# Gated loads and merged attention events in a decay-attention and softplus-FFN kernel

## The chip, the cores and the metric

The kernel runs on 1 core of a Trainium2 chip. The metric is the device time of one execution in microseconds, the median of several runs. Before the change it is 607.69 us (three runs, 607.14 to 608.19).

## The reference

An attention with exponential decay, without softmax, computed in blocks of 64 positions with a carried state, feeds a two-layer network with a softplus between the layers. All is float32: q, k and v are 4 x 8 x 768 x 64 (batch, heads, positions, size of a head), the network maps 512 to 2048 to 512 for 3072 tokens.

```python
for b in range(nb):
    qb, kb, vb = q[:, :, sl], k[:, :, sl], v[:, :, sl]
    intra = np.einsum('bhic,bhjc->bhij', qb, kb) * Dmask[None]
    intra = np.einsum('bhij,bhjd->bhid', intra, vb)
    inter = np.einsum('bhid,bhde->bhie', qb * lam_pow[None], kv_state)
    out[:, :, sl] = intra + inter
    kb_dec = kb * rev_pow[None]
    kv_state = lam_block[None, :, None, None] * kv_state + np.einsum('bhsd,bhse->bhde', kb_dec, vb)
...
h = x @ w_in
g = np.maximum(h, 0.0) + np.log1p(np.exp(-np.abs(h)))
return (g @ w_out).astype(np.float32)
```

## The kernel before

**Units and chunks.** Positions go in 6 chunks of 128, heads in 4 pairs; a chunk and a pair make one of 24 attention *units* (`NG`), unit g being pair g % 4 of chunk g // 4. Each has its q, k, transposed k and v in one tile of 1 MB, loaded by two transfers of 512 KB (L84, `load_upto`). For a unit, `k_decay` (ACT) and `q_decay` (DVE) scale the inputs; `mm_scores` on PE makes the scores x and the state increments y in 64x64 matmuls (L307, L309); `mask_scores` on DVE (L334) multiplies by the decay mask; `update_states` on DVE (L339) carries the states. `mm_out` (L322, L326) then makes the output in `z`, which `x_high` (ACT, L371) and `x_low` (DVE, L378) split into a high and a low part.

**The network.** It goes in 96 steps, one for each of 16 slices of the 2048 hidden features in each of 6 chunks. `mlp1(s)` (L406) makes h for step s by twelve 128x512 matmuls (4 pairs, three products of high and low parts); `chain_act`, `chain_hi` (ACT, L387, L391) and `chain_lo` (DVE, L395) take the softplus and split it; `mlp2` (L423) of the same step, twelve matmuls more, comes four steps later (`LAG`) and adds into four output banks of its chunk. At a chunk's end the banks are copied out (L429) and stored (L431).

**Weights.** There are 32 raw weight blocks of 512 KB (L126, `w_load`), in the order of `w_order`: first the inner weights of steps 0 to 3, then outer and inner ones in turn. Each is rounded and split on the chip, two at a time in the loop: `w_scale`, `w_round` (ACT, L213, L217), `w_shift`, `w_sign`, `w_add` (DVE, L221, L225, L231), then, one step later, `w_hi` (ACT, L234) and `w_lo` (DVE, L238). Blocks 2s and 2s + 1 begin at step s; the last pair begins at step 15. `w_lo` at step s finishes the outer weight that `mlp2` of step s - 3 needs.

**Order.** The order of the instructions on each engine is that of the program; waits between engines are put in where tiles are shared. Up to step 3 of the loop the order is a list written out by hand (L461 to L473): `xy p` is `mm_scores` of unit p, `a` the mask, `st` the copy of its states, `dg` and `sl` carry them, `z` is `mm_out`, `warm n` is n idle matmuls, `load n` and `unit n` call `w_load(n)` and `load_upto(n)`. All loads are issued by SP in the order of the program; an issue waits there until its tile is free.

**The loop** (L485 on) runs over s from 4. In each step, in the order of the program: the decays of a unit whose event is at s + 1; softplus and split of step s - 1; `w_hi` of the old pair of weights, `w_scale` and `w_round` of the new one, `w_lo` of the old, `w_shift`, `w_sign`, `w_add` of the new; `mlp2` of step s - 4; the attention events; `mlp1(s)`; the loads. Events are of three kinds:

- separate scores (`scores_at`, steps 6, 9, 12 and 17 for units 5 to 8): scores and masks lie in the two banks of `work`;
- separate outputs (`outs_at`, steps 5, 8, 11 and 14 for units 4 to 7);
- both at once (`both_at`, from step 19 every four steps, for the scores of units 9 to 23 and the outputs of the unit before): `mm_out(g - 1)` goes into `work`, and x and y take the two banks of pool `h`, which `mlp1` uses too; a second `mlp2` of the next slice follows, and the next step has none.

The accumulators take all eight PSUM banks: four of `o`, two of `work`, two of `h`.

```python
def work(name):
    return ps.tile([128, 2, 512], F32, tag="t", bufs=1, name=name)
def bank(name):
    return ps.tile([128, 512], F32, tag="h", bufs=2, name=name)
```

Of the kernel before, what the change touches and what calls it, by code (L numbers as in the profile page):

```python
# [7 lines left out]
F32 = mybir.dt.float32  # L8
# [6 lines left out]
B, H, S, D = 4, 8, 768, 64  # L15
C = 128
T = 64
NCH = S // C
NP = H // 2
NG = NCH * NP  # L20
DM = H * D
DFF = 2048
NF = DFF // 128
# [8 lines left out]
def decay_attention_softplus_ffn(  # L32
# [7 lines left out]
    nc = tc.nc  # L40
    ctx.enter_context(tc.manual_schedule())
    cp = ctx.enter_context(tc.tile_pool(name="cp", bufs=1))
# [37 lines left out]
    def load_upto(n):  # L80
        for g in range(len(units), min(n, NG)):
            t = t8([128, 2, 2, 512], F32, f"att{g}")
            for major in range(2):
                nc.sync.dma_start(out=t[:, major], in_=att[g // NP, g % NP, :, major])  # L84
            units.append(t)
# [19 lines left out]
    def keep_values(g):  # L105
        v = t2([128, B, 2, D], F32, f"v_{g}")
        nc.scalar.copy(out=v, in_=part(g, 1, 1))
        values[g] = v
# [10 lines left out]
    def w_load(n):  # L119
        nonlocal n_raw  # L120
        while n_raw < min(n, NW):
            k = n_raw
            if k % 2 == 0:
                raws[k] = raws[k + 1] = t8([128, 2, DM, 2], U32, f"raw{k}")
            f, which = w_order[k]
            nc.sync.dma_start(  # L126
                out=raws[k][:, k % 2].rearrange("q n t -> q (n t)"), in_=wts[f, which].bitcast(U32)
            )
            n_raw += 1

    for n in range(NP - 1):
        load_upto(n + 1)
        w_load(n + 1)
    load_upto(NP)
    w_load(7)
    load_upto(NP + 1)


    spare = t8([128, 4, 512], F32, "spare")
# [116 lines left out]
    lo, hi = half(0), half(1)  # L256
# [13 lines left out]
    def own(g, n, name):  # L270
        if not first_chunk(g):
            return t2([128, B, 2, 64], F32, f"{name}_{g}")
        if g not in spares:
            spares[g] = t8([128, 3, B, 2, 64], F32, f"own_{g}")
        return spares[g][:, n]

    def k_decay(g):
        kd = kds[g] = own(g, 0, "kd")
        if g == 0:
            w = rp1[:, heads(g)].rearrange("q (o t w) -> q o t w", o=1, w=1).broadcast_to([128, B, 2, D])  # L280
            nc.vector.tensor_mul(out=kd, in0=kt_of(g), in1=w)
            return
        for t in range(2):
            h = heads(g).start + t
            nc.scalar.activation(kd[:, :, t], kt_of(g)[:, :, t], AF.Copy, scale=rp1[:, h : h + 1])  # L285

    def q_decay(g):
        qd = qds[g] = own(g, 1, "qd")
        r = hi if first_chunk(g) else slice(0, 128)
        eng = nc.gpsimd if g < 2 else nc.vector  # L290
        w = lp[r, heads(g), :].rearrange("q (o t) i -> q o (t i)", o=1).broadcast_to([r.stop - r.start, B, 2 * T])
        eng.tensor_mul(
            out=qd[r].rearrange("q b t i -> q b (t i)"), in0=q_of(g)[r].rearrange("q b t i -> q b (t i)"), in1=w
        )
# [102 lines left out]
    def mlp1(s, ps_=range(NP)):  # L397
        c, f = divmod(s, NF)
        if s not in h_tiles:
            h_tiles[s] = bank(f"h{s}")  # L400
        w = w_of(f, 0)
        for p in ps_:
            cs = slice(p * 128, (p + 1) * 128)
            x = x_of(c, p)
            for n, (i, j) in enumerate(((0, 0), (1, 0), (0, 1))):
                nc.tensor.matmul(  # L406
                    h_tiles[s], lhsT=w[:, i, cs], rhs=x[:, j, :],
                    start=p == 0 and n == 0, stop=p == NP - 1 and n == 2,
                )

    def mlp2(ss):
        c = ss[0] // NF
        ends = ss[-1] % NF == NF - 1
        if ss[0] % NF == 0:
            o_tiles[c] = [obank(f"o{c}_{b}") for b in range(B)]
        if ends:
            ob = t8([128, B, 512], F32, f"ob{c}")
        for b in range(B):
            for s in ss:
                f = s % NF  # L420
                g, w = g_tiles[s], w_of(f, 1)
                for n, (i, j) in enumerate(((0, 0), (0, 1), (1, 0))):
                    nc.tensor.matmul(  # L423
                        o_tiles[c][b], lhsT=g[:, i, b * 128 : (b + 1) * 128], rhs=w[:, j],
                        start=f == 0 and n == 0, stop=f == NF - 1 and n == 2,
                    )
            if ends:
                copy = nc.vector.tensor_copy if b % 2 else nc.scalar.copy
                copy(out=ob[:, b], in_=o_tiles[c][b])  # L429
                queue = nc.scalar if c == NCH - 1 and b % 2 == 0 else nc.sync  # L430
                queue.dma_start(out=out[b * S + c * C : b * S + (c + 1) * C, :], in_=ob[:, b])  # L431
# [4 lines left out]
    def scores_of(g):  # L436
        w = work(f"w{g}")
        mm_scores(g, w[:, 0], w[:, 1])
        mask_scores(g, w[:, 0])
        update_states(g, w[:, 1])  # L440
# [8 lines left out]
    def end(p):  # L449
# [6 lines left out]
        "dg": lambda p: carry_states(p, xy[p][1]), "sl": lambda p: next_states(p, xy[p][1]), "xh": lambda p: x_high(p, z[p]),  # L456
        "xl": lambda p: x_low(p, z[p]), "scale": w_scale, "round": w_round, "shift": w_shift, "sign": w_sign,
        "add": w_add, "hi": w_hi, "lo": w_lo, "act": chain_act, "ghi": chain_hi, "glo": chain_lo,
        "mlp": lambda s, *ps_: mlp1(s, ps_ or range(NP)), "scores": scores_of, "load": w_load, "unit": load_upto, "warm": keep_warm,
    }  # L460
    for line in """  # L461
        q 0, k 0, xy 0, scale 0, round 0, a 0, st 0, q 1, warm 3, shift 0, sign 0, z 0, add 0, k 1, xh 0,
        xl 0, hi 0, xy 1, dg 0, scale 1, lo 0, st 1, a 1, q 2, round 1, mlp 0 0, warm 4, sl 0, shift 1,
        sign 1, z 1, add 1, k 2, xy 2, dg 1, xh 1, xl 1, hi 1, scale 2, round 2, lo 1, a 2, st 2, sl 1, q
        3, mlp 0 1, warm 4, load 8, shift 2, sign 2, add 2, k 3, z 2, xy 3, xh 2, xl 2, hi 2, scale 3,
        round 3, shift 3, a 3, st 3, lo 2, sign 3, dg 2, mlp 0 2, warm 2, add 3, z 3, mlp 1 0, mlp 1 1,
        mlp 1 2, scale 4, round 4, xh 3, hi 3, sl 2, xl 3, shift 4, lo 3, sign 4, add 4, load 10, mlp 0 3,
        mlp 1 3, scale 5, round 5, q 4, k 4, act 0, ghi 0, hi 4, shift 5, sign 5, add 5, lo 4, dg 3, mlp
        2, act 1, ghi 1, hi 5, glo 0, glo 1, lo 5, scale 6 7, round 6 7, scores 4, unit 6, load 12, act 2,
        ghi 2, mlp 3, glo 2, sl 3, shift 6 7, sign 6 7, add 6 7  # L470
    """.replace("\n", " ").split(","):
        name, *numbers = line.split()
        step[name](*map(int, numbers))  # L473
# [2 lines left out]


    last = NCH * NF
    scores_at = {3 * n + 3: NP + n for n in range(NP)}
    outs_at = {s + 2: g for s, g in scores_at.items()}  # L480
    scores_at[NF + 1] = 2 * NP
    both_at = {4 * g - 17: g for g in range(2 * NP + 1, NG)}
    outs_at[4 * NG - 17] = NG - 1
    units_at = {**scores_at, **both_at}
    for s in range(LAG, last + LAG):  # L485
        if s + 1 in units_at:
            k_decay(units_at[s + 1])
            q_decay(units_at[s + 1])
        if s - 1 < last:
            chain_act(s - 1)  # L490
            chain_hi(s - 1)
            chain_lo(s - 1)
        old, new = w_group(s - 1), w_group(s)
        if old:
            w_hi(*old)
        if new:
            w_scale(*new)
            w_round(*new)
        if old:
            w_lo(*old)  # L500
        if new:
            w_shift(*new)
            w_sign(*new)
            w_add(*new)
        if s == last + LAG - 2:
            mlp2([s - LAG, s - LAG + 1])
        elif s - LAG < last - 1 and s - 1 not in both_at:
            mlp2([s - LAG])
        if s in scores_at:
            scores_of(scores_at[s])  # L510
            if scores_at[s] == 2 * NP:
                keep_values(2 * NP)
        if s in both_at:

            g = both_at[s]
            w, x, y = work(f"z{g - 1}"), bank(f"x{g}"), bank(f"y{g}")
            mm_out(g - 1, w)
            mm_scores(g, x, y)
            mask_scores(g, x)
            x_high(g - 1, w)  # L520
            update_states(g, y)
            x_low(g - 1, w)
            if g < NG - 1:
                keep_values(g)
            mlp2([s + 1 - LAG])
        if s in outs_at:
            g = outs_at[s]
            w = work(f"z{g}")
            mm_out(g, w)
            x_high(g, w)  # L530
            x_low(g, w)
        if s < last:
            mlp1(s)
        w_load(2 * s + (8 if s < 9 else 6))
        if s in units_at:
            load_upto(units_at[s] + 2)


def _layout(q, k, v, lam, w_in, w_out):
# [37 lines left out]
```

## Time and profile before

| What | Value |
|---|---|
| median of three runs | 607.69 us |
| the profiled execution | 607.95 us |
| its span, first to last instruction | 606.2 us |
| DVE busy, share of the span | 226.4 us, 37% |
| ACT busy, share of the span | 219.8 us, 36% |
| read from HBM, written | 41.95 MB, 6.29 MB |
| mean granted clock of TensorE | 0.999 |

The profile is of one execution. Its page gives each engine's busy time, the span in 40 slices, the DMA queues, the chain of work that ended last and the costliest groups of instructions. PE is TensorE's matmuls, PEld its weight loads, DVE VectorE, ACT ScalarE, SP the engine that issues the loads. L with a number is a line of the kernel, `out<-in` the tiles of an instruction with their numbers left out. The timeline lists instructions with their start and length in us, merged where they follow one another; in brackets stands the engine's idle time before, and what ended it ("issue": nothing that the profile shows). A windows row gives a stretch, its length, each engine's busy time with the count of its instructions (PE, PEld, DVE, ACT, POOL), the granted clock, the DMA engines' busy share and GB/s; a row for one engine has that engine alone.

### The profile page before, as it was taken

The page shows a single profiled execution, that of the slowest core. Times are in us where ns is not written, and L with a number is a line of the kernel's source. Part 1 is how long each engine was busy: PE and PEld are TensorE (multiplying, and loading weights), DVE is VectorE, ACT ScalarE, POOL GpSimd, SP SyncE. Part 2 cuts the span into 40 slices and gives each one's busy share as a digit, 9 for nine tenths or more (in the row PEclk, how much of TensorE's full clock was granted, in tenths as well). Part 3 has the DMA queues.
Part 4 walks back from the last instruction along what each step waited for, and adds up shares of the span by engine and source line. Part 5 has one row for each costly group of instructions (what it writes and reads, how often), then busy time and mean ns, then how long its engine had stood idle before and what let it go on. Part 6 is the DMA issues. An engine that isn't in the chain of part 4 may idle for free.

```text
span 606.2 us, 11776 instructions
## 1 busy us (share of the span) xinstructions
PE 596.9 (98%) x5299; PEld 488.5 (81%) x5299; DVE 226.4 (37%) x336; ACT 219.8 (36%) x355; POOL 4.7 (1%) x11
## 2 busy tenths in 40 slices
PE   9899999999999999999999999999999999999997
PEld 6577888888888888888888888888888888888886
DVE  7779999853232233132222321321312211211111
ACT  3777777633222223332223323222333121322121
POOL 3000000000000000000000000000000000000000
PEclk9999999999999999999999999999999999999999
DMA  8995314216002023300120500211500000100001
GB/s 297 406 406 227 122 74 141 88 52 208 3 2 70 1 70 98 112 2 11 61 70 29 182 2 0 71 32 40 207 3 1 1 1 1 69 2 0 1 0 69
DMA packets 15169, 48.98 MB, mean 81 GB/s; under 512 B 1808, under 2 KB 1808, under 8 KB 15120
## 3 DMA queue, kind: packets, MB, share of 16 engines
q1 hardware_dynamic: 14832, 47.72, 21.8%
q8 instruction: 41, 0.67, 0.4%
q10 hardware_dynamic: 288, 0.52, 0.2%
q14 instruction: 8, 0.07, 0.0%
HBM read 41.95 MB, written 6.29 MB: 80 GB/s over the span
## 4 chain that ended last, share of the span: by engine, by line
PE 91%; DMA 7%; DVE 1%; SPq 1%; ACT 0%; issue 0%
PE o L423 43%; PE h L406 41%; DMA raw<-in_wts 5%; PE z L322 2%; PE x L307 2%; DMA att<-in_att 2%; PE z L326 2%; PE w L307 1%; PE y L309 1%; SPq L84 0%; DVE w L238 0%; DVE c L231 0%; DVE c L225 0%; SPq L126 0%; ACT w L234 0%; PE w L309 0%
## 5 line engine op out<-in xcount | busy, mean ns | idle before, releaser
L423 PE MATMUL o<-w,g 128*128 128x512 f32 x1152 | 278.9, 391 | 1.1 <-DVE w L238 0.8
L406 PE MATMUL h<-x,w 128*128 128x512 f32 x1152 | 276.8, 391 | 0.0
L423 PEld LDWEIGHTS o<-w,g 128*128 128x128 f32 x1152 | 215.0, 188 | 47.2 <-DVE w L238 1.1
L406 PEld LDWEIGHTS h<-x,w 128*128 128x128 f32 x1152 | 215.1, 188 | 46.7 <-issue 1.2
L395 DVE TENSOR_TENSOR g<-l,g 128x512 fp32r<-128x512 f32 x96 | 66.4, 692 | 310.4 <-ACT g L391 310.2
L387 ACT ACTIVATE l<-h 128x512 f32<-128x512 f32 x96 | 57.4, 598 | 309.0 <-PE h L406 306.4
L391 ACT CAST g<-l 128x512 fp32r<-128x512 f32 x96 | 59.6, 621 | 3.1
L371 ACT CAST x<-z 128x512 fp32r<-128x512 f32 x24 | 14.0, 585 | 41.4 <-PE z L326 41.4
L334 DVE TENSOR_TENSOR a<-x,mask 128x512 f32<-128x512 f32 x15 | 10.4, 692 | 36.1 <-PE y L309 26.4
L339 DVE SCALAR_TENSOR_TENSOR st<-st,lam_c,y 64x256 f32<-64x256 f32 x52 | 22.9, 480 | 0.8
L322 PEld LDWEIGHTS z<-qd,st 64*64 64x64 f32 x640 | 17.0, 134 | 7.0 <-issue 7.0
L307 PE MATMUL x<-att 64*64 64x64 f32 x608 | 21.9, 219 | 0.0
L213 ACT ACTIVATE c<-raw 128x1024 f32<-128x1024 f32 (+1 forms) x19 | 19.0, 1001 | 7.3 <-DMA raw<-in_wts 7.3
L234 ACT CAST w<-c 128x1024 fp32r<-128x1024 f32 (+1 forms) x19 | 17.4, 914 | 10.3 <-DVE c L231 7.7
L238 DVE TENSOR_TENSOR w<-c,w 128x1024 fp32r<-128x1024 f32 (+1 forms) x19 | 20.0, 1053 | 2.8 <-ACT w L234 2.7
L231 DVE CUSTOM_DVE_ANT_0 c<-raw,c 128x2048 uint16<-128x2048 uint16 (+1 forms) x19 | 20.1, 1058 | 2.4
L322 PE MATMUL z<-qd,st 64*64 64x64 f32 x640 | 20.9, 224 | 0.0
L307 PEld LDWEIGHTS x<-att 64*64 64x64 f32 x608 | 20.0, 135 | 1.0 <-PE z L326 0.5
L225 DVE SCALAR_TENSOR_TENSOR c<-raw,c 128x1024 uint32<-128x1024 uint32 (+1 forms) x19 | 20.1, 1056 | 0.6
L378 DVE TENSOR_TENSOR x<-z,x 128x512 fp32r<-128x512 f32 x24 | 16.6, 690 | 7.9 <-ACT x L371 7.5
L217 ACT ACTIVATE raw<-raw 128x1024 uint32<-128x1024 uint32 (+1 forms) x19 | 18.9, 993 | 0.0
L285 ACT ACTIVATE kd<-att,rp 128x256 f32<-128x256 f32 x40 | 18.1, 502 | 0.0
(54 smaller groups left out, 230.5 us busy)
## 6 DMA issues: line engine op xcount, KB each, us to landing
att<-in_att SPq DMA_DIRECT2D x48, 512.0 KB, 5.5
raw<-in_wts SPq DMA_DIRECT2D x32, 512.0 KB, 10.2
out_dram<-ob SPq DMA_DIRECT2D x22, 256.0 KB, 2.2
out_dram<-ob ACTq DMA_DIRECT2D x2, 256.0 KB, 2.0
lam_b<-in_lam SPq DMA_DIRECT2D x1, 4.0 KB, 2.6
```

Source lines behind the costliest of these rows:

```text
L213: nc.scalar.activation(c.bitcast(F32), raw_at(ks, 1).bitcast(F32), AF.Copy, scale=2.0**-112)
L225: nc.vector.scalar_tensor_tensor(out=c, in0=raw_at(ks, 1), scalar=0x80000000, in1=c, op0=ALU.bitwise_and, op1=ALU.bitwise_or)
L231: nc.vector.tensor_add(out=c, in0=c, in1=raw_at(ks, 0))
L238: nc.vector.tensor_sub(out=w[:, 1], in0=conv.pop(ks[0]).bitcast(F32), in1=w[:, 0])
L307: nc.tensor.matmul(x[r, cols], lhsT=k[r, b, t], rhs=q[r, b, t], start=True, stop=True)
L322: nc.tensor.matmul(w[half(t), s, cols], lhsT=st[r, b, t], rhs=qd[r, b, t], start=True, stop=False)
L339: nc.vector.scalar_tensor_tensor(out=to[:, :, t], in0=of[:, :, t], scalar=lam_c[r, h : h + 1], in1=u[:, :, t], op0=ALU.mult, op1=ALU.add,)
L387: nc.scalar.activation(l_tiles[s], h_tiles.pop(s), AF.Softplus)
L391: nc.scalar.copy(out=g_tiles[s][:, 0, :], in_=l_tiles[s])
L395: nc.vector.tensor_sub(out=g[:, 1, :], in0=l_tiles.pop(s), in1=g[:, 0, :])
L406: nc.tensor.matmul(h_tiles[s], lhsT=w[:, i, cs], rhs=x[:, j, :], start=p == 0 and n == 0, stop=p == NP - 1 and n == 2,)
L423: nc.tensor.matmul(o_tiles[c][b], lhsT=g[:, i, b * 128 : (b + 1) * 128], rhs=w[:, j], start=f == 0 and n == 0, stop=f == NF - 1 and n == 2,)
```

## The change

1. Before the list only units 0 to 3 and weights 0 to 2 are issued (before: 0 to 6 and unit 4 as well), unit 3 now ahead of weight 2.
2. `fence` is new: a store of 16 bytes, issued by SP, from a tile into a small tile `marks`. SP waits there until the tile has been written, and so do all loads behind it. `fk p` reads the decayed k of unit p, `fs p` its states, `fg s` the high part of step s. In the list they gate weights 3 and 4 (`fk 2`), 5 (`fs 2`), unit 4 (`fk 3`), weights 6 and 7 (`fs 3`), 8 (`fg 0`), unit 5 with 9 and 10 (`fg 1`), and 11 (`fg 2`). Unit 4 thereby goes ahead of weights 6 and 7.
3. In the list `warm 4` behind `mlp 0 1` and `warm 2` behind `mlp 0 2` are gone, `act 0` goes ahead of `round 5`, and `q 4, k 4` go behind `lo 4`.
4. The separate events are gone. Units 5 to 8 have both at once, at steps 6, 9, 12 and 15, by the code that served units 9 to 23. v of units 6 and 7 is now copied as well (`keep_values`).
5. The last bank of the output is copied in two halves, by ACT and by DVE, each stored by SP.

```diff
-    for n in range(NP - 1):
+    for n in range(2):
         load_upto(n + 1)
         w_load(n + 1)
     load_upto(NP)
-    w_load(7)
-    load_upto(NP + 1)
+    w_load(3)
+    marks = cp.tile([128, 32], F32, name="marks")
+    n_marks = 0
+    def fence(ap):
+        nonlocal n_marks
+        nc.sync.dma_start(out=marks[64:65, 4 * n_marks : 4 * n_marks + 4], in_=ap)
+        n_marks += 1
...
-            if ends:
+            if ends and c == NCH - 1 and b == B - 1:
+                for n, copy in enumerate((nc.scalar.copy, nc.vector.tensor_copy)):
+                    cols = slice(n * 256, (n + 1) * 256)
+                    copy(out=ob[:, b, cols], in_=o_tiles[c][b][:, cols])
+                    nc.sync.dma_start(out=out[b * S + c * C : b * S + (c + 1) * C, cols], in_=ob[:, b, cols])
+            elif ends:
...
+        "fk": lambda p: fence(own(p, 0, "kd")[64:65, 0, 0, 0:4]), "fs": lambda p: fence(states[p][64:65, 0, 0, 0:4]),
+        "fg": lambda s: fence(g_tiles[s][64:65, 0, 0:4].bitcast(F32)), "warm": keep_warm,
...
-        sign 1, z 1, add 1, k 2, xy 2, dg 1, xh 1, xl 1, hi 1, scale 2, round 2, lo 1, a 2, st 2, sl 1, q
-        3, mlp 0 1, warm 4, load 8, shift 2, sign 2, add 2, k 3, z 2, xy 3, xh 2, xl 2, hi 2, scale 3,
-        round 3, shift 3, a 3, st 3, lo 2, sign 3, dg 2, mlp 0 2, warm 2, add 3, z 3, mlp 1 0, mlp 1 1,
-        mlp 1 2, scale 4, round 4, xh 3, hi 3, sl 2, xl 3, shift 4, lo 3, sign 4, add 4, load 10, mlp 0 3,
-        mlp 1 3, scale 5, round 5, q 4, k 4, act 0, ghi 0, hi 4, shift 5, sign 5, add 5, lo 4, dg 3, mlp
-        2, act 1, ghi 1, hi 5, glo 0, glo 1, lo 5, scale 6 7, round 6 7, scores 4, unit 6, load 12, act 2,
-        ghi 2, mlp 3, glo 2, sl 3, shift 6 7, sign 6 7, add 6 7
+        sign 1, z 1, add 1, k 2, fk 2, load 5, xy 2, dg 1, xh 1, xl 1, hi 1, scale 2, round 2, lo 1, a 2,
+        st 2, fs 2, load 6, sl 1, q 3, mlp 0 1, shift 2, sign 2, add 2, k 3, fk 3, unit 5, z 2, xy 3, xh
+        2, xl 2, hi 2, scale 3, round 3, shift 3, a 3, st 3, fs 3, load 8, lo 2, sign 3, dg 2, mlp 0 2,
+        add 3, z 3, mlp 1 0, mlp 1 1, mlp 1 2, scale 4, round 4, xh 3, hi 3, sl 2, xl 3, shift 4, lo 3,
+        sign 4, add 4, mlp 0 3, mlp 1 3, scale 5, act 0, round 5, ghi 0, fg 0, load 9, hi 4, shift 5, sign
+        5, add 5, lo 4, q 4, k 4, dg 3, mlp 2, act 1, ghi 1, fg 1, unit 6, load 11, hi 5, glo 0, glo 1, lo
+        5, scale 6 7, round 6 7, scores 4, act 2, ghi 2, fg 2, load 12, mlp 3, glo 2, sl 3, shift 6 7,
+        sign 6 7, add 6 7
...
-    scores_at = {3 * n + 3: NP + n for n in range(NP)}
-    outs_at = {s + 2: g for s, g in scores_at.items()}
-    scores_at[NF + 1] = 2 * NP
-    both_at = {4 * g - 17: g for g in range(2 * NP + 1, NG)}
-    outs_at[4 * NG - 17] = NG - 1
-    units_at = {**scores_at, **both_at}
+    both_at = {3 * g - 9: g for g in range(NP + 1, 2 * NP + 1)}
+    both_at.update({4 * g - 17: g for g in range(2 * NP + 1, NG)})
...
-        if s in scores_at:
-            scores_of(scores_at[s])
-            if scores_at[s] == 2 * NP:
-                keep_values(2 * NP)
...
-            if g < NG - 1:
+            if NP + 1 < g < NG - 1:
                 keep_values(g)
             mlp2([s + 1 - LAG])
-        if s in outs_at:
-            g = outs_at[s]
+        if s == 4 * NG - 17:
+            g = NG - 1
```

More of the change, by code (lines that the diff above doesn't have):

```diff
@@ L458, in decay_attention_softplus_ffn @@
         "add": w_add, "hi": w_hi, "lo": w_lo, "act": chain_act, "ghi": chain_hi, "glo": chain_lo,
-        "mlp": lambda s, *ps_: mlp1(s, ps_ or range(NP)), "scores": scores_of, "load": w_load, "unit": load_upto, "warm": keep_warm,
+        "mlp": lambda s, *ps_: mlp1(s, ps_ or range(NP)), "scores": scores_of, "load": w_load, "unit": load_upto,
+        "fk": lambda p: fence(own(p, 0, "kd")[64:65, 0, 0, 0:4]), "fs": lambda p: fence(states[p][64:65, 0, 0, 0:4]),
+        "fg": lambda s: fence(g_tiles[s][64:65, 0, 0:4].bitcast(F32)), "warm": keep_warm,
     }
@@ L478, in decay_attention_softplus_ffn @@
     last = NCH * NF
-    scores_at = {3 * n + 3: NP + n for n in range(NP)}
-    outs_at = {s + 2: g for s, g in scores_at.items()}
-    scores_at[NF + 1] = 2 * NP
-    both_at = {4 * g - 17: g for g in range(2 * NP + 1, NG)}
-    outs_at[4 * NG - 17] = NG - 1
-    units_at = {**scores_at, **both_at}
+    both_at = {3 * g - 9: g for g in range(NP + 1, 2 * NP + 1)}
+    both_at.update({4 * g - 17: g for g in range(2 * NP + 1, NG)})
     for s in range(LAG, last + LAG):
-        if s + 1 in units_at:
-            k_decay(units_at[s + 1])
-            q_decay(units_at[s + 1])
+        if s + 1 in both_at:
+            k_decay(both_at[s + 1])
+            q_decay(both_at[s + 1])
         if s - 1 < last:
@@ L534, in decay_attention_softplus_ffn @@
         w_load(2 * s + (8 if s < 9 else 6))
-        if s in units_at:
-            load_upto(units_at[s] + 2)
+        if s in both_at:
+            load_upto(both_at[s] + 2)
 def _layout(q, k, v, lam, w_in, w_out):
```

## The prediction

> **What bounds the kernel now.** I read the page first, then windows, then three timelines. From the page:
>
> ```profile
> PE 596.9 (98%) x5299; PEld 488.5 (81%) x5299; DVE 226.4 (37%) x336; ACT 219.8 (36%) x355; POOL 4.7 (1%) x11
> ...
> q8 instruction: 41, 0.67, 0.4%
> ```
>
> PE is busy 98% of the span, so on the whole it is the bound. But the average hides two stretches: DVE, 37% on average, is nearly full while weights are still converted (a row below), and in the first 31 us PE's time is broken by holes.
>
> The holes, from a window over PE (its matmuls, clock, DMA share and GB/s) and from PE's timeline (idle time in brackets):
>
> ```profile
> 24.23:30.70 6.48, 5.04 (x127) 1.00 1.02 406
> ```
> ```profile
> 24.23 0.21 PE L322 MATMUL z<-own,st 64*64 64x64 f32 x1 [0.55 <-issue]
> ...
> 30.71 0.36 PE L326 MATMUL z<-own,att 64*64 64x64 f32 x9 [1.44 <-issue]
> ```
>
> PE stops in the middle of `mm_out`, between matmuls of one form that wait for nothing, the second 127 matmuls after the first. 41 instruction packets of 0.67 MB are 16 KB each, and 5299 matmuls with as many weight loads make 258 instructions a packet, 129 pairs. So I read these stops as PE waiting for its next block of code, fetched while loads keep the DMA engines full (share 1.02). A block of 128x512 matmuls alone would last 127 x 0.227 = 29 us (2.72 for twelve, by a row below); the attention's small ones use one up in 5.04 us busy, which is why the stops sit here. The two stops cost 0.55 and 1.44 us, with the 0.21 us that the view still credits to the last matmul 0.76 and 1.65.
>
> **The change, part by part.**
>
> *Startup.* Loads behind unit 3 now wait on SP for markers: tiny stores that read `kd` of unit 2, `st` of unit 2, and so on. What is queued behind each marker is only later loads. The queue's rows:
>
> ```profile
> 6.67 0.33 SPq L126 DMA_DIRECT2D raw<-in_wts  x1
> ...
> 26.07 11.82 SPq L126 DMA_DIRECT2D raw<-in_wts  x10
> ```
> ```profile
> DMA to landing us min/median/max: 11.7/11.7/11.7
> ```
>
> The first row is weight 2; the last, of that issue alone, says that it lands at 18.4. Ten issues in 11.82 us, each held for an earlier landing, give (11.82 - 0.33)/9 = 1.28 us for each 512 KB. The new order puts both halves of unit 3 ahead of weight 2, so that lands at 18.4 + 2.56 = 20.95. Then the engines run dry but for what markers release. ACT's timeline says who notices:
>
> ```profile
> 20.08 0.69 ACT L213 ACTIVATE c<-raw 128x512 f32<-128x512 f32 x1
> 20.66 0.68 ACT L217 ACTIVATE raw<-raw 128x512 uint32<-128x512 uint32 x1
> 21.36 0.58 ACT L347 COPY st<-y 64x512 f32<-64x512 f32 x1
> ...
> 27.39 0.58 ACT L347 COPY st<-y 64x512 f32<-64x512 f32 x1
> ...
> 31.55 0.59 ACT L371 CAST x<-z 128x512 fp32r<-128x512 f32 x1 [2.30 <-PE z L326]
> ```
>
> `scale 2` moves from 20.08 to about 20.95, so `st 2` ends at 21.36 + 0.58 + 0.87 = 22.8 and `z 2` cannot start before. Four warming matmuls ahead of `z 2` are gone, but that start leaves little of their time, and the code behind the stop that ends at 24.23 is fetched while loads are queued up to 20.95 and weights 3 and 4 follow: I leave that stop nearly as it is (0 to 0.75 us gained). The next block is asked for near 24, when only weight 5 and unit 4 are under way: stop gone, 1.65. Two more warming matmuls are gone ahead of `z 3`: 2 x 0.227 = 0.45, which `st 3` permits (it ends at 27.97; the stop within `z 3` began at 30.71 - 1.65 = 29.06). Sum 2.1 to 2.85; **I take 2.5 us**. Bounds: 0, if the stops stay; 3.8, if both go with all six warming matmuls (0.76 + 1.65 + 6 x 0.227). What is late next: ACT and DVE wait for `z 3` at 31.55, so the rest of the startup moves with it. By the order written out, each marked load is released one or more stages ahead of its use; weights 8 and 9, behind the gates of steps 0 and 1 and scaled in loop step 4, have the least room. A marker's own landing holds up nobody.
>
> The Trainium skill ("Runtime: NRT & Kernel Launch", section "Instruction fetch mechanics") says that code comes in 16 KiB blocks of 256 instructions, which agrees with 127 and 16 KB here, and that crossing a block is "mostly hidden", which speaks against this gain; by that the startup would bring 0 and the sum would be the first rival's. The traced stops, only at block ends, decide against it.
>
> *Merged events.* Outs of units 4 to 7 and scores of 5 to 8, eight separate events, become four (s = 6, 9, 12, 15). What PE alone saves, from windows of one period each:
>
> ```profile
> 60.74:79.70 18.96, 18.96 (x207) 15.41 (x201) 18.37 (x23) 14.59 (x20) 0.00 (x0) 1.00 0.27 99
> ...
> 189.84:213.87 24.03, 24.03 (x230) 19.92 (x224) 6.52 (x11) 6.79 (x13) 0.00 (x0) 1.00 0.14 45
> ```
> ```profile
> 48.89 1.24 DVE w L238
> 50.13 0.04 issue
> ...
> 63.76 2.72 PE o L423 x12
> ```
>
> Twelve matmuls take 2.72, a step 5.44. The old period is three steps and both events apart: 18.96 - 16.32 = 2.64. A merged one (second row) is four steps: 24.03 - 21.76 = 2.27; so 0.37 us saved an event, 1.5 in all. But the first row also shows DVE busy 18.37 of 18.96 (third busy figure): it has no room. Now DVE's timeline at the scores of unit 5, with PE and ACT:
>
> ```profile
> 59.42 0.68 DVE L395 TENSOR_TENSOR g<-l,g 128x512 fp32r<-128x512 f32 x1
> 60.03 1.23 DVE L238 TENSOR_TENSOR w<-c,w 128x1024 fp32r<-128x1024 f32 x1
> 61.17 0.69 DVE L221 TENSOR_SCALAR c<-c 128x1024 uint32<-128x1024 uint32 x1
> 61.89 1.23 DVE L225 SCALAR_TENSOR_TENSOR c<-raw,c 128x1024 uint32<-128x1024 uint32 x1
> 63.26 1.23 DVE L231 CUSTOM_DVE_ANT_0 c<-raw,c 128x2048 uint16<-128x2048 uint16 x1
> 64.40 0.69 DVE L334 TENSOR_TENSOR a<-w,mask 128x512 f32<-128x512 f32 x1
> ```
> ```profile
> 60.74 3.02 PE L406 MATMUL h<-x,w 128*128 128x512 f32 x12
> 63.59 2.88 PE L423 MATMUL o<-w,g 128*128 128x512 f32 x12
> ```
> ```profile
> 63.79 0.60 ACT L387 ACTIVATE l<-h 128x512 f32<-128x512 f32 x1 [1.67 <-PE h L406]
> 64.42 0.62 ACT L391 CAST g<-l 128x512 fp32r<-128x512 f32 x1
> 64.95 1.05 ACT L234 CAST w<-c 128x1024 fp32r<-128x1024 f32 x1
> ```
>
> PE finished these scores at 60.74; the mask (L334) came at 64.40, queued on DVE behind the step's conversions. Today that hurts nobody: separate scores lie in `work`, and `mlp1` takes a bank of pool `h`. A merged event takes both banks of `h` for x and y, so `mlp1(s)` behind it must wait for the mask, and who waits next is its softplus, `chain_lo`, and DVE's whole queue. DVE's work is on the path, in a ring:
>
> - mask's end to `mlp1` 0.04 (50.13 to 50.17), `mlp1` 2.85 (60.74 to 63.59), to its softplus 0.20: 3.09.
> - Softplus start to `w_hi`'s end 64.95 + 1.05 - 63.79 = 2.21, handoff 0.03: 2.24. Then `w_lo`, shift, sign, add, by starts 60.03 to 64.40: 4.37.
> - Next step: `q_decay` 0.6 (as `chain_lo`, of the same size), `chain_lo` 0.61, and 4.37 again: 5.58.
> - Third step: `w_lo` waits for `w_hi`, which starts only behind the add: 0.09 + 0.02 + 1.05, 1.16; 4.37 again; mask 0.69: 6.22.
>
> Together 3.09 + 2.24 + 4.37 + 5.58 + 6.22 = **21.5 us a round**, where PE alone would need 18.6. State updates and `x_low` lie beside `mlp1`. Bounds: 18.6 (nothing waits) and 22 (0.5 for handoffs that I misjudge); I take 21.5, as each piece is a row's.
>
> The first merged mask stands where the old one did, ending at 65.1: its `x_low` is no longer ahead, but `w_lo` then waits for `w_hi` about as long. The fourth ends three rounds later, 129.6. Then `mlp1(15)` 2.85, `mlp1(16)`, `mlp2(13)`, `mlp1(17)` 2.72 each: `mlp2(14)` starts at 140.6. Before:
>
> ```profile
> 131.35 0.39 PE L423 MATMUL o<-w,g 128*128 128x512 f32 x1
> ```
>
> So 9.2 us later, with the 1.5 us saved already in it; from there both programs run alike. Two more `keep_values` on ACT lie beside PE.
>
> *End.* The last 128x512 copy becomes two halves on ACT and DVE, both stored by SP.
>
> ```profile
> 602.49 0.69 DVE L429 COPY ob<-o 128x512 f32<-128x512 f32 x1 [2.03 <-PE o L423]
> ```
>
> If halves run together: about 0.35 saved, less 0.33 for the second issue (an issue's time in SP's rows above); one behind the other (both read one bank): about 0.2 lost. I take 0, between -0.4 and +0.4.
>
> **The sum.** Against the profiled execution (607.95 us, its span 606.2 and 1.75 around it): 607.95 + 9.2 - 2.5 = 614.65. The median of the runs, 607.69, is 0.26 lower: **614.4 us**, slower by 1.1%.
>
> **The rivals.**
> 1. *Startup brings nothing* (stops have another cause, or later fetches meet the released loads). For: loads still fill the DMA engines at the first of them. Against: their spacing of 127. 607.7 + 9.2 = 616.9.
> 2. *PE pauses but DVE catches up.* Each `mlp1` waits 1.3 us (the second `mlp2` of the event waits for `w_lo`, 60.03 + 1.23 = 61.3, and ends some 2.5 later, at 63.8, against the mask's 65.1), without the ring. For: DVE's backlog clears by itself in plain steps. Against: 18.37 of 18.96 busy. 607.7 - 2.5 - 1.5 + 5.2 = 608.9.
> 3. *Faster: the mask does not hold `mlp1`.* If DVE reaches the mask before PE has ended the second `mlp2` (decisive point: mask done within 2.8 us of the scores; today it is 4.35, 60.74 to 65.09), only savings stay: 607.7 - 2.5 - 1.5 = 603.7. For: events from s = 19 do so, but no conversions remain there.
> That the markers release nothing too early is the same as rival 1.
>
> **How the numbers follow.** Forecast 0.66 (its own range 612.4 to 616.4: the startup between 2.0 and 3.0, three rounds off by up to 0.5 each), rival 1 0.10, rival 2 0.10, rival 3 0.14. The range 608.8 to 617.4 takes in the forecast, rival 1 and the upper half of rival 2, and leaves out rival 3. A measurement of this kernel can tell about 0.2%, 1.2 us. Faster 0.14 (rival 3); same 0.03 (the lower part of rival 2); slower 0.83.
>
> **What would show it.** Right: `mlp1` behind the merged events at s = 6, 9, 12 starts when the mask ends, with over 1 us of idle PE before it, and these masks stand 21.5 us apart; DVE idles before `chain_lo` after each event; the stop near 30 us is gone and `xh 3` comes near 29. Wrong: masks 18.6 to 19 us apart, no idle PE at the events, or stops of PE still 127 matmuls apart.

## The result, and the profile after

The changed kernel takes 614.27 us (median of four runs, 614.09 to 614.45) against 607.67 us before: slower, by a ratio of 1.0107 with a 95% interval of 1.0094 to 1.0120. The forecast was 614.4 us. The profiled execution takes 614.09 us, its span 612.3.

Here are the two large groups of matmuls on the page of the kernel before, then the span and the same groups on the page of the changed kernel. The last column is PE's idle time ahead of them and what ended most of it:

```profile
L423 PE MATMUL o<-w,g 128*128 128x512 f32 x1152 | 278.9, 391 | 1.1 <-DVE w L238 0.8
L406 PE MATMUL h<-x,w 128*128 128x512 f32 x1152 | 276.8, 391 | 0.0
```
```profile
span 612.3 us, 11792 instructions
...
L431 PE MATMUL o<-w,g 128*128 128x512 f32 x1152 | 282.0, 393 | 4.3 <-DVE w L246 4.0
L414 PE MATMUL h<-x,w 128*128 128x512 f32 x1152 | 275.6, 390 | 4.2 <-DVE a L342 4.2
```

`mlp1` (now L414) is kept waiting by the mask (`a`, L342), `mlp2` (L431) by `w_lo` (L246). Both waits can be seen in the first merged event, s = 6. DVE's timeline of the changed kernel there:

```profile
59.94 1.23 DVE L239 CUSTOM_DVE_ANT_0 c<-raw,c 128x2048 uint16<-128x2048 uint16 x1
61.08 0.68 DVE L342 TENSOR_TENSOR a<-x,mask 128x512 f32<-128x512 f32 x1
61.80 1.79 DVE L347 SCALAR_TENSOR_TENSOR st<-st,lam_c,y 64x256 f32<-64x256 f32 x4
63.62 0.69 DVE L386 TENSOR_TENSOR x<-z,x 128x512 fp32r<-128x512 f32 x1
66.20 0.69 DVE L403 TENSOR_TENSOR g<-l,g 128x512 fp32r<-128x512 f32 x1 [1.89 <-ACT g L399]
```

PE's timeline at the same place:

```profile
57.18 0.51 PE L431 MATMUL o<-w,g 128*128 128x512 f32 x1
57.99 2.79 PE L431 MATMUL o<-w,g 128*128 128x512 f32 x11 [0.31 <-DVE w L246]
61.82 3.51 PE L414 MATMUL h<-x,w 128*128 128x512 f32 x14 [1.04 <-DVE a L342]
```

PE is through with the scores at 57.18, where the second `mlp2` of the event begins. The mask comes at 61.08, directly behind the last conversion (L239), ends at 61.76, and `mlp1` starts at 61.82. Then DVE, which had almost no idle time to give, itself waits 1.89 us for the softplus of that `mlp1`. The ring closes in the next masks, rows of the same DVE timeline:

```profile
82.73 0.68 DVE L342 TENSOR_TENSOR a<-x,mask 128x512 f32<-128x512 f32 x1
...
104.32 0.68 DVE L342 TENSOR_TENSOR a<-x,mask 128x512 f32<-128x512 f32 x1
...
125.86 0.69 DVE L342 TENSOR_TENSOR a<-x,mask 128x512 f32<-128x512 f32 x1
```

From 61.08 on they stand 21.65, 21.59 and 21.54 us apart. Before the change the masks of the separate scores came every 18.6; behind the one at 64.40, in DVE's timeline of the kernel before:

```profile
83.03 0.68 DVE L334 TENSOR_TENSOR a<-w,mask 128x512 f32<-128x512 f32 x1
...
101.66 0.68 DVE L334 TENSOR_TENSOR a<-w,mask 128x512 f32<-128x512 f32 x1
```

The startup gained. ACT's `x_high` of unit 3, at 31.55 before, now comes here (ACT's timeline):

```profile
28.07 0.59 ACT L379 CAST x<-z 128x512 fp32r<-128x512 f32 x1
```

3.5 us earlier. `mlp2(14)`, where the prediction closed its account, starts here (PE's timeline):

```profile
137.62 0.39 PE L431 MATMUL o<-w,g 128*128 128x512 f32 x1
```

137.62 against 131.35: 6.3 us later. So the loop lost 6.3 + 3.5 = 9.8 us, the startup gave back 3.5, and the last 0.2 came from the end.

### The profile page after: what moved, and what is told of

It reads as the page before. It is cut to its first block, busy times and chain, and to the rows that moved or that the text cites. A ratio compares the mean times of both kernels' runs of the same rounds, so it can differ in the third digit from the quotient of the medians.

```text
span 612.3 us, 11792 instructions
## 1 busy us (share of the span) xinstructions
PE 597.0 (98%) x5293; PEld 486.1 (79%) x5293; DVE 227.5 (37%) x336; ACT 220.5 (36%) x358; POOL 4.1 (1%) x11
## 4 chain that ended last, share of the span: by engine, by line
PE 81%; DVE 7%; DMA 4%; ACT 4%; issue 3%; SPq 0%; DVEq 0%; ACTq 0%
PE h L414 38%; PE o L431 37%; DMA raw<-in_wts 4%; DVE c L239 3%; PE x L315 2%; PE z L330 2%; DVE c L233 2%; PE z L334 1%; ACT w L242 1%; DVE c L229 1%; ACT raw L225 1%; ACT l L395 1%; PE y L317 1%; DVE w L246 1%; ACT c L221 0%
## 5 line engine op out<-in xcount | busy, mean ns | idle before, releaser
L431 PE MATMUL o<-w,g 128*128 128x512 f32 x1152 | 282.0, 393 | 4.3 <-DVE w L246 4.0
L414 PE MATMUL h<-x,w 128*128 128x512 f32 x1152 | 275.6, 390 | 4.2 <-DVE a L342 4.2
L414 PEld LDWEIGHTS h<-x,w 128*128 128x128 f32 x1152 | 215.4, 188 | 52.1 <-DVE a L342 5.9
L431 PEld LDWEIGHTS o<-w,g 128*128 128x128 f32 x1152 | 214.2, 188 | 53.6 <-DVE w L246 8.0
L347 DVE SCALAR_TENSOR_TENSOR st<-st,lam_c,y 64x256 f32<-64x256 f32 x68 | 29.9, 480 | 1.1
L342 DVE TENSOR_TENSOR a<-x,mask 128x512 f32<-128x512 f32 x19 | 13.1, 690 | 36.3 <-PE y L317 26.6
L315 PE MATMUL x<-att 64*64 64x64 f32 x736 | 26.6, 219 | 0.0
L315 PEld LDWEIGHTS x<-att 64*64 64x64 f32 x736 | 24.3, 135 | 1.0 <-issue 0.5
L221 ACT ACTIVATE c<-raw 128x1024 f32<-128x1024 f32 (+1 forms) x19 | 18.9, 997 | 8.4 <-DMA raw<-in_wts 8.4
L246 DVE TENSOR_TENSOR w<-c,w 128x1024 fp32r<-128x1024 f32 (+1 forms) x19 | 20.0, 1055 | 3.8 <-ACT w L242 3.7
L317 PE MATMUL y<-att,kd 64*64 64x64 f32 x544 | 21.3, 219 | 0.0
L239 DVE CUSTOM_DVE_ANT_0 c<-raw,c 128x2048 uint16<-128x2048 uint16 (+1 forms) x19 | 20.1, 1057 | 2.4
L317 PEld LDWEIGHTS y<-att,kd 64*64 64x64 f32 x544 | 19.6, 135 | 0.0
L225 ACT ACTIVATE raw<-raw 128x1024 uint32<-128x1024 uint32 (+1 forms) x19 | 18.9, 994 | 0.0
```

Of the source, the lines that this page charges most:

```text
L239: nc.vector.tensor_add(out=c, in0=c, in1=raw_at(ks, 0))
L246: nc.vector.tensor_sub(out=w[:, 1], in0=conv.pop(ks[0]).bitcast(F32), in1=w[:, 0])
L315: nc.tensor.matmul(x[r, cols], lhsT=k[r, b, t], rhs=q[r, b, t], start=True, stop=True)
L317: nc.tensor.matmul(y[half(1 - s), cols], lhsT=kd[r, b, t], rhs=v[r, b, t], start=s == 0 or not first_chunk(g), stop=s == 0 or not first_ch ...
L347: nc.vector.scalar_tensor_tensor(out=to[:, :, t], in0=of[:, :, t], scalar=lam_c[r, h : h + 1], in1=u[:, :, t], op0=ALU.mult, op1=ALU.add,)
L414: nc.tensor.matmul(h_tiles[s], lhsT=w[:, i, cs], rhs=x[:, j, :], start=p == 0 and n == 0, stop=p == NP - 1 and n == 2,)
```

## Experiments

Each was run beside the kernel before, on the same chip as it; ratios are to that.

### Each half of the change alone

The first run has the changed startup and end with the old loop (`scores_at`, `outs_at`); the second the old startup with the merged loop and the new end. Against the changed kernel, the first and then the second:

```diff
-    both_at = {3 * g - 9: g for g in range(NP + 1, 2 * NP + 1)}
-    both_at.update({4 * g - 17: g for g in range(2 * NP + 1, NG)})
+    scores_at = {3 * n + 3: NP + n for n in range(NP)}
+    outs_at = {s + 2: g for s, g in scores_at.items()}
+    scores_at[NF + 1] = 2 * NP
+    both_at = {4 * g - 17: g for g in range(2 * NP + 1, NG)}
...
```
```diff
-    for n in range(2):
+    for n in range(NP - 1):
...
-    w_load(3)
+    w_load(7)
+    load_upto(NP + 1)
...
```

> The changed kernel's startup, markers and split last copy, with the old loop (separate events). Theory (ring through the mask and the h banks costs 9.6 us in the loop, startup gives 3.4, last copy 0.2): 607.7 - 3.6 = 604.1 us. Rival (the markers release weights too late and starve the conversions in the loop, the merging is harmless): the loss stays with the markers, 612 us or more.

> The old startup (no markers, warming matmuls kept), with the merged events and the split last copy. Theory: the loop's loss stands alone, 607.7 + 9.6 - 0.2 = 617.1 us, merged masks 21.6 us apart. Rival (late weights are the loss): merging then only saves, 606 us.

Measured: 604.98 us (ratio 0.9955, 0.9940 to 0.9970) and 617.03 us (1.0156, 1.0139 to 1.0173). The loss is the merged loop's alone, and the startup is a gain. The rival, late weights, falls as the main cause, but has a share of about 0.6 in the 0.9 us that the first run stays over its expectation. Its DVE and ACT timelines at loop step 4:

```profile
47.07 0.69 DVE L229 TENSOR_SCALAR c<-c 128x1024 uint32<-128x1024 uint32 x1 [0.58 <-ACT c L221]
```
```profile
45.91 1.13 ACT L221 ACTIVATE c<-raw 128x1024 f32<-128x1024 f32 x1 [0.67 <-DMA raw<-in_wts]
```

The scaling of weights 8 and 9 waits 0.67 us for their load, and DVE 0.58 us behind it. These were the two with the least room. From unit 3's `x_high` to `mlp2(14)` this run takes 100.4 us, where the kernel before takes 99.8: the 0.6 is not made up again.

### The scores' banks alone

The kernel before, with nothing merged and no markers; only the separate scores of units 5 to 8 move from `work` to the two banks of `h`:

```diff
     def scores_of(g):
-        w = work(f"w{g}")
-        mm_scores(g, w[:, 0], w[:, 1])
+        if g > NP:
+            x, y = bank(f"x{g}"), bank(f"y{g}")
+        else:
+            w = work(f"w{g}")
+            x, y = w[:, 0], w[:, 1]
+        mm_scores(g, x, y)
...
```

> The kernel before, with one thing changed: the separate scores of units 5 to 8 lie in the two banks of pool h, not in work. Nothing is merged, no markers. Theory (the banks make the ring): mlp1 behind the scores waits for the mask, masks of units 5 to 7 stand 21.5 apart instead of 18.6, about 617 us. Rival (merging itself is what costs): as before, 607.7 us.

Measured: 624.80 us (1.0284, 1.0268 to 1.0299). The two banks make such a ring by themselves, with nothing merged: holding `mlp1`'s banks until a late mask is what costs. But it costs almost 8 us more than expected, with masks 24.2 us apart. The reason stands in PE's timeline and two windows over all engines of that run (the first figure behind the brackets is the granted clock):

```profile
65.03 0.62 PE L406 MATMUL h<-x,w 128*128 128x512 f32 x1 [4.30 <-DVE a L334]
```
```profile
65.00:71.50 6.50, 6.47 (x21) 5.19 (x22) 2.30 (x5) 1.79 (x3) 0.00 (x0) 0.74 0.00 0
...
89.20:94.00 4.80, 4.79 (x14) 3.85 (x15) 1.75 (x4) 0.18 (x1) 0.00 (x0) 0.65 0.61 218
```

Here no second `mlp2` stands between the scores and `mlp1`, so PE is idle for 4.30 us, and behind that the clock is granted at 0.74 only. `mlp1` takes 4.60 us there, where one at full clock took 3.02, and all that waits for it comes later by that. This is 1.6 of the 2.6 us by which a round is longer than in the changed kernel; the rest is not taken apart here.

### The mask ahead of the conversions

The changed kernel; in event steps the conversions of the new pair come behind the event on DVE:

```diff
-        if new:
-            w_shift(*new)
-            w_sign(*new)
-            w_add(*new)
+        if s not in both_at:
+            convert()
...
             x_low(g - 1, w)
+            convert()
```

> The changed kernel with one move on DVE: in the steps with a merged event, shift, sign and add of the new weights come behind the mask, the states and x_low, not ahead. Theory (what costs is the mask's place behind the conversions while it holds the banks of mlp1): masks come 18.6 to 18.9 us apart, no wait of mlp1 on the mask, 602.5 to 604.5 us. Rival (PE pauses at the mask but DVE catches up, so only the four pauses of 1.43 come back): 608.5 us. Rival (DVE is simply too full for four events by step 15, wherever the mask stands): 613 us or more.

Measured: 608.49 us (1.0017, 1.0008 to 1.0027). 5.8 us come back from the changed kernel's 614.27, which is the number of the rival that spoke of pauses only; the theory's 602.5 to 604.5 is missed. Its DVE timeline shows two masks:

```profile
57.88 0.68 DVE L342 TENSOR_TENSOR a<-x,mask 128x512 f32<-128x512 f32 x1
...
78.14 0.68 DVE L342 TENSOR_TENSOR a<-x,mask 128x512 f32<-128x512 f32 x1
```

They are 20.26 apart: neither 21.6 nor the 18.6 of my theory. PE's timeline says why:

```profile
58.02 2.78 PE L431 MATMUL o<-w,g 128*128 128x512 f32 x11 [0.31 <-DVE w L246]
60.64 5.60 PE L414 MATMUL h<-x,w 128*128 128x512 f32 x24
66.08 0.39 PE L431 MATMUL o<-w,g 128*128 128x512 f32 x1
67.07 1.67 PE L431 MATMUL o<-w,g 128*128 128x512 f32 x6 [0.60 <-DVE w L246]
```

`mlp1` (60.64) no longer waits, but `mlp2` still does. A merged event brings forward a second `mlp2`, of step s - 3, whose weight `w_lo` finishes in the very step of the event; apart, it came a step later. That is a second way round the ring, only 1.4 us a round shorter than the one through the mask. So DVE did not simply catch up, as that rival has it: its total fits, its mechanism does not.

### Events first, and one mlp2 a step

The next run takes both links away: in the four early events, outputs, scores, mask, states and `x_low` come right behind `chain_lo`, the conversions behind them, and each step has its one `mlp2`.

```diff
             chain_lo(s - 1)
+        early = s in both_at and s < NF
+        if early:
+            event(s)
...
-        elif s - LAG < last - 1 and s - 1 not in both_at:
+        elif s - LAG < last - 1 and (s - 1 not in both_at or s <= NF):
...
+        if s in both_at and not early:
+            event(s)
             mlp2([s + 1 - LAG])
```

> The changed kernel; in the four early events (s = 6 to 15) the order is: chain_lo, then outputs and scores, mask, states and x_low, then the conversions, and one mlp2 in each step (none doubled, none left out). Theory after the first runs (two links make the ring: mlp1 behind the mask, and the event's second mlp2 behind the w_lo of the same step): neither link is left, masks 18.6 to 18.9 us apart, no wait of mlp2 on w_lo after step 5, 602 to 603.5 us. Rival (DVE is too full for four events and the conversions, so 20.2 a round is its floor): 608 us.

Measured: 605.65 us (0.9971, 0.9960 to 0.9981). The floor of 20.2 is refuted, but my 18.6 to 18.9 is missed too: the masks come 19.3 apart. Its DVE timeline has one wait left in a round:

```profile
64.77 1.23 DVE L246 TENSOR_TENSOR w<-c,w 128x1024 fp32r<-128x1024 f32 x1 [0.51 <-ACT w L242]
```

That is the term of the predicted ring in which `w_lo` waits for `w_hi`, which cannot start before DVE's add has ended. So the last of these runs puts work there: `x_low` of the event moves one step on, between `chain_lo` and `w_lo`.

```diff
-        x_low(g - 1, w)
+        if s < NF - 1:
+            late[s + 1] = g - 1, w
+        else:
+            x_low(g - 1, w)
...
             chain_lo(s - 1)
+        if s in late:
+            x_low(*late[s])
```

> The run with the events first, and x_low of the events at s = 6, 9 and 12 moved into the next step, between chain_lo and w_lo. Theory (what is left there, 19.3 a round, is DVE's own work of 18.7 and its wait of 0.5 to 0.6 for w_hi, which x_low now fills): rounds 18.6 to 18.8, that wait gone, 605.65 - 4 x 0.6 = 603.3 us. Rival (PE or ACT sets the 19.3): no change, 605.6 us.

Measured: 604.31 us (0.9942, 0.9930 to 0.9955), 1.3 us less of the 2.4 expected. Two masks in its DVE timeline:

```profile
56.68 0.69 DVE L342 TENSOR_TENSOR a<-x,mask 128x512 f32<-128x512 f32 x1
...
75.33 0.69 DVE L342 TENSOR_TENSOR a<-x,mask 128x512 f32<-128x512 f32 x1
```

18.65 apart, and that is DVE's own work: its timeline shows no wait between these masks, so no more is to be had by order. Of what is missing, 0.6 is a miscount: `x_low` moves in three of the four events, and four masks have three rounds between them, not four. About 0.6 more went at step 4, where ACT waits 0.90 us for weights 8 and 9 (0.30 in the run before). That wait differs between runs that share the changed startup: 0.18, 0.30, 0.38, 0.67 and 0.90 us in five traces.

### What stops PE in the startup

The kernel before with 12 tiny matmuls added ahead, then the kernel before without the six warming matmuls:

```diff
     keep_warm(18)
+    for _ in range(12):
+        nc.tensor.matmul(warm_ps[:64, :64], lhsT=warm[:, :64], rhs=warm[:, :64], start=True, stop=True)
```
```diff
-        3, mlp 0 1, warm 4, load 8, shift 2, sign 2, add 2, k 3, z 2, xy 3, xh 2, xl 2, hi 2, scale 3,
-        round 3, shift 3, a 3, st 3, lo 2, sign 3, dg 2, mlp 0 2, warm 2, add 3, z 3, mlp 1 0, mlp 1 1,
+        3, mlp 0 1, load 8, shift 2, sign 2, add 2, k 3, z 2, xy 3, xh 2, xl 2, hi 2, scale 3,
+        round 3, shift 3, a 3, st 3, lo 2, sign 3, dg 2, mlp 0 2, add 3, z 3, mlp 1 0, mlp 1 1,
```

> The kernel before with 12 tiny 64x64 matmuls added behind the first warming ones. Theory (PE stops at the end of a block of code): the stops come after the same count of matmuls as before, 221, 348 and 475, and so 12 matmuls earlier in the work than before. Rival (PE waits there for data or for a certain instruction): the stops stay in the same place of the work, at counts 233, 360 and 487.

> The kernel before, without the same six warming matmuls, nothing else. Theory (PE then only reaches the end of its code block earlier and stops longer): the stops grow by what the warming matmuls took, 607.2 to 607.7 us. Rival (the warming matmuls were on the path): 607.5 - 1.4 = 606.1 us.

The stops can be counted: windows over PE alone, first from the start to the end of a stop, then from there to the end of the next. With 12 matmuls more:

```profile
1.40:23.62 22.23, 20.98 (x348) 1.00 0.96 356
23.62:29.82 6.19, 5.05 (x127) 1.00 1.03 408
```

Without the warming ones:

```profile
1.40:23.90 22.50, 19.37 (x348) 1.00 0.96 356
23.90:30.35 6.45, 4.70 (x127) 1.00 1.03 410
```

348 and 127 in both, though the same count lies 12 matmuls earlier in the work in the one and four to six later in the other. PE stops at a count and not at a fixed place of the work, which is what blocks of code that run out would do. (At 221, the first, the added matmuls leave a wait for `st` in the same place, so that one proves nothing.)

The DMA queues of the traces bear it out. The instruction queue (q8) moves one packet, 16 KB, at 21.6 and one at 28.1 us in the kernel before; PE's stops end 2.6 us behind each, at 24.23 and 30.71. With 12 matmuls more they come at 21.1 and 27.2, without the warming ones at 21.5 and 27.9, and there the stops end 2.4 to 2.6 us behind them.

The run with 12 matmuls more takes 608.11 us, in one execution. Without the six matmuls the two stops end idle times of 1.48 and 1.76 us, longer than the 0.55 and 1.44 before, and the time stays: 607.75 us (1.0010, 0.9999 to 1.0021). The warming matmuls were free, because PE waited behind them anyway.

Last, the markers with the warming matmuls put back (`warm 4` behind `mlp 0 1`, `warm 2` ahead of `add 3`; old loop, as in the first run):

> The run with the old loop (markers, split last copy), with the six warming matmuls put back. Theory (the markers remove PE's stops by clearing the DMA engines for its code; the warming matmuls are a separate, smaller term): the stops near 24 and 30 us stay away, 605.0 + 0.8 = 605.8 us. Rival (taking out the warming matmuls is what gained): back to 607.5 us.

Measured: 605.41 us (0.9970, 0.9957 to 0.9982), against 604.98 without them; the difference is within the spread. There is no stop near 24 or 30 us. Its ACT timeline at unit 3's `x_high`:

```profile
28.45 0.59 ACT L379 CAST x<-z 128x512 fp32r<-128x512 f32 x1 [0.59 <-PE z L334]
```

28.45 against 31.55 before: the gated loads in their new order, with the warming matmuls kept, bring 3.1 of the startup's 3.5 us. In the first run, without the warming matmuls, this `x_high` starts at 27.95, so with the stops gone they may cost 0.5.

### The versions that beat both kernels

The late `x_low` with weight 2 ahead of unit 3 again; and the old loop with that and with weight 9 released together with weight 8 (`ghi 0, fg 0, load 10`):

```diff
-    load_upto(NP)
-    w_load(3)
+    load_upto(NP - 1)
+    w_load(3)
+    load_upto(NP)
```

> The run before in this call, with weight 2 issued ahead of unit 3 again, as in the kernel before. Theory (PE's wait for st 2 near 22 us, 0.7, comes from weight 2 behind unit 3): that wait goes, 0.5 to 0.9 us less, 602.6 us. Rival (unit 3 then comes later and costs as much): 603.3 us or more.

> The run with the old loop (markers, split last copy, separate events), with weight 2 ahead of unit 3 and weight 9 released one marker earlier, with weight 8. Theory: the wait for st 2 goes (0.6), and the late scaling of weights 8 and 9 with DVE's wait near 47 us (0.6): 605.0 - 1.2 = 603.8 us. Rival (both are hidden by what follows): 605.0 us.

Measured: 603.71 us (0.9936, 0.9924 to 0.9949) and 603.63 us (0.9938, 0.9925 to 0.9952), where 602.6 and 603.8 were expected. DVE's wait at step 4 is gone in both, though only the second releases weight 9 earlier. Both beat both kernels, and by the same amount. That does not make merging worthless: from unit 3's `x_high` to `mlp2(14)` the merged run takes 99.1 us (28.30 to 127.40) and the one with separate events 99.8 (27.34 to 127.14). With its rings undone, merging saves 0.7 us by these two traces, of the 1.5 that PE alone would save. The merged run's startup is later by more than that, 0.6 of it at the first stop (it ends at 18.03 against 17.41), which differs between runs without a change there.

## Why the prediction was right

Its sum was right to 0.1 us, its terms less so, and that is partly luck: the loop cost 0.6 us more, the startup gained 1.0 more and the end 0.2. Profile against profile the change is 6.1 us where the sum has 6.7; that the medians differ by 6.6 is the spread of the runs.

**The loop (9.2 predicted, 9.8 measured).** The mechanism is as predicted: masks 21.6 apart for 21.5, `mlp1` starting when the mask ends, DVE idle before `chain_lo`. That the banks make this ring, even with nothing merged, is shown by the scores in `h`. What the prediction left out is the second link, from `w_lo` to the event's second `mlp2`. It priced that only as a detail of rival 2, and said that without the mask's hold "only savings stay". In the changed kernel the mask comes last, so the sum did not suffer from it; but with the mask's hold taken away and nothing else, the run took 608.49 us and not rival 3's 603.7. The runs show the pieces: 5.8 us for the mask's place, 2.8 more for the second link with the order of the event, 1.3 or somewhat more for `w_lo` behind `w_hi`.

**The startup (2.5 predicted, 3.5 measured).** The step that failed is "I leave that stop nearly as it is". The stop at 24.23 went as well. Windows over PE in the changed kernel (the last two figures are the DMA engines' share and GB/s):

```profile
18.10:19.10 1.00, 1.00 (x39) 1.00 0.35 131
```

Loads were to fill the DMA engines up to 20.95, and weights 3 and 4 to follow without a break. In fact the share is 0.35 already between 18.1 and 19.1, though the load of weight 2 lands only about 20.7, where ACT's scaling of it starts; weights 3 and 4 are issued from 18.11 on, behind the first marker. The packet of code for this stop goes through at 18.7, 1.0 us behind the end of the stop before it (17.68), and not at 21.6, 3.5 us behind (18.11), as in the kernel before. The next comes at 23.7, about where the prediction had it. What took the stop's place is the wait that was predicted, in PE's timeline:

```profile
22.56 0.27 PE L330 MATMUL z<-own,st 64*64 64x64 f32 x2 [0.74 <-ACT st L355]
```

`z 2` begins at 22.56 (22.8 predicted, from weight 2 behind unit 3). What that wait costs was not measured cleanly. With weight 2 back in front, the run with the late `x_low` takes 0.6 us less, as expected, but its runs before lay between 602.93 and 604.85. By the traces, unit 3's `x_high` even starts 0.40 later there (28.30 against 27.90), with a stop of 0.16 us idle at the count of 475; what it gained is DVE's wait at step 4, 0.81 us before. That code is fetched late beside full loads, and not "mostly hidden" as the Trainium skill ("Runtime: NRT & Kernel Launch", "Instruction fetch mechanics") puts it, is what the counted stops, the packets of code and the markers' run show together. So rival 1 is refuted.

**The end (0 predicted).** DVE's and ACT's last copies, with SP's issues between them:

```profile
608.85 0.37 ACT L439 COPY ob<-o 128x256 f32<-128x256 f32 x1 [0.77 <-PE o L431]
609.24 0.81 SPq L440 DMA_DIRECT2D out_dram<-ob  x2
609.25 0.42 DVE L439 COPY ob<-o 128x256 f32<-128x256 f32 x1 [2.43 <-ACT ob L439]
```

The halves run one behind the other. The last copy ends 0.82 us after the first one's start, where the whole copy took 0.69. The smaller last store may make up for it: 128 KB land in 1.7 us, where 256 KB took 2.0. By the two spans the end is 0.2 us shorter; it was not run by itself.

**The rivals.** Rival 3 (faster) fails at its own deciding point: the mask ended 4.6 us after the scores, not within 2.8. Rival 2's number (608.9) was met by a run, 608.49, whose trace shows another mechanism. A total that fits a theory did not make it right.

Left open: why the first stop, at 221 matmuls, and the wait for weights 8 and 9 vary from run to run without a change there. Totals that lie within about 1 us of each other can differ by these two alone.

## What to carry to other kernels

Before merging two steps for the sake of the engine that is busiest, look at what each of the two shared buffers with, and in whose queue its release stands: here a bank moved from a pool that nobody waited for to one that the next matmuls need, and its release stood behind 3 us of other work on an engine that was 37% busy on average and 97% in that stage. Take both links of such a ring out before judging it; with one gone, the next longest showed almost at once. And read two equal totals by their stages before calling two orders equal. Where loads run far ahead of their use, holding them back can pay through what shares the DMA engines with them, code among it.

## What was not expected of the hardware

- Small matmuls use up a block of code in about 5 us, and beside full loads (share 1.02 to 1.03) the next block comes too late: stops of 0.55 to 1.76 us idle, each at the same count of matmuls (348, then 127 more) in three kernels, and each ending 2.4 to 2.6 us behind a 16 KB packet of the instruction queue.
- A pause of 4.30 us cost PE its clock: 0.74 granted in the 6.5 us behind it, 0.65 in the 4.8 us behind the next, of 3.56 us. The pauses of 1.04 us in the changed kernel left it at 1.0. The Trainium skill ("TensorE: Matmul & The Clock Gate", "What's actually happening") gives an idle window of about 3.4 us for the fall to half rate; the pauses of 4.30 and 3.56 us lie above it, those of 1.04 us below.
